# Places moved in a hand-written order of work: visits of attention tiles by one or two products, and three actions of tile 1

## The chip, the cores and the metric

The kernel runs on one core of a Trainium2 chip. The metric is the device time of one execution in microseconds (us), the median of several runs. The engines are TensorE (PE in the profile, its weight loads PEld), VectorE (DVE), ScalarE (ACT), GpSimd (POOL) and SyncE (SP, which here only issues DMAs).

## The reference

Attention over blocks, then a gated feed-forward network (FFN) over all its rows:

```python
batch, n_heads, seq, head_dim = 8, 8, 576, 64      # q, k, v
scores = q @ k.T / sqrt(64)
scores = where(pos_i // 64 >= pos_j // 64, scores, -1e9)   # causal by blocks of 64
attn_out = softmax(scores) @ v

x = attn_out.transpose(0, 2, 1, 3).reshape(4608, 512)
out = (maximum(x @ w_gate, 0) * (x @ w_val)) @ w_out       # 512 -> 1536 -> 512
```

Inputs and output are float32; the kernel works in bfloat16 with sums in float32.

## The kernel before, in words

**Tiles.** Each of the eight batches gives 576 rows of x. The first 512 of a batch are one tile of the FFN (tiles 0 to 7). The last 64 of all batches, their tails, make tile 8.

**FFN.** The generator `ffn_gen` (L931) issues the FFN's matmuls one by one. For each of a tile's 12 blocks of the hidden width there are four products of x with the gate weights (into a PSUM bank `ffnp`), whose relu is done by ScalarE (L947), and four with the value weights (into another `ffnp`), which VectorE multiplies with the relu (`hidden`, L957, tile `hT`). The product with w_out follows. In tiles 0 and 1 it takes 48 matmuls; from tile 2 on it is done by a scheme of seven half-size products, 42 places in place of 48. So a tile is 144 places in tiles 0 and 1, and 138 from tile 2 on: 96 of the gate and value products, then 42. Tile 7's gate and value products are done by a scheme of their own.

**Attention beside it.** While the FFN of tile j runs, the four pairs of heads of batch j + 1 (rounds r = 4b to 4b + 3) are computed between its products. A round has these actions:
- `s`, the *visit* (L431 to L470): the scores of both heads of the pair. They go into two tiles `sc` of two banks each and into a third piece, which is one bank `one` for one head and one bank `ffnp` for the other. The visit begins with this third piece. Then ScalarE makes the exp of the third piece (two instructions, L466) and of the first `sc` (L459).
- `e`: the exp of the second `sc`; `c`: zeros into the corners of the masked blocks (by VectorE in nearly all rounds).
- `a` and `b`: the products with V of the first and the second head (L551), each behind it normalised by VectorE: a reciprocal, a multiplication into `xnat` (L528) and, from batch 3 on, one into `xtail` (L535).
- `x`: `xnat` is transposed into the next tile's `xT`, by a DMA (L633) or, in the first batches, by TensorE through a PSUM bank and a copy (`to_xT_pe`, L625 to L631).

In PSUM there are two `sc` tiles, one bank `one`, and three banks `ffnp`. The gates, the values, the products with V and half of each visit's third piece take turns at the `ffnp` banks.

**Early batches.** Batches 0 to 2 are loaded, cast and transposed by other ways. `cast_tails` (L204) casts tails of k and v from a staging tile into `k_bt` and `v_bf`; `td1` is its part for one half of the heads of batch 1, done by VectorE: one cast of k and one of v. `pe_tails` (`t1`, L289 to L304) transposes the tails of q and k on TensorE. `unpermute` (`u2`, L253 to L257) copies q and k of one pair of heads of batch 2 into their places (`qTm`, `kTm`), here by two VectorE copies. Actions named `q`, `ev`, `tc`, `v2` are GpSimd's casts for these batches; GpSimd issues its own DMAs in between.

**What sets the order.** The program writes all engines' instructions in an order made by hand. The table `AT` (L1325) gives each action a place counted in the FFN's places. The loop at its end sorts the actions by place, lets the FFN run up to the place and then issues the action; an action's instructions thereby get their position on every engine at once. For batches 4 to 7 (which run beside tiles 3 to 6) the places come from `STEADY` (L1608), an offset within a round of 28 places (loop L1701 to L1708). `place_of` (L1735) rounds down and, from tile 2 on, shortens the last 48 places of each 144 to 42.

```python
STEADY = {"s": 2, "e": 8, "c": 15, "a": 22, "b": 26, "x": 26.1}
...
for n in sorted(acts, key=lambda n: AT[n]):
    at = int(place_of(AT[n]))
    ffn(at - place[0])          # FFN matmuls up to here
    place[0] = max(place[0], at)
    acts[n]()                   # then the action
```

Of the kernel before, what the change touches and what calls it, by code (L numbers as in the profile page):

```python
# [17 lines left out]
def kernel(  # L18
# [287 lines left out]
    def load_qkv(b, which, behind=None):  # L306
        for t in which:
            src = (q, k, v)[t]
            for c in range(NCH):
                if (b, 0) not in bfs:  # L310
                    bfs[b, 0], bfs[b, 1] = new_bf(), new_bt()
                here = src[b, :, 128 * c : min(128 * c + 128, S), :]
                if c < 4:
                    dst = (
                        v_bf[b % 2][:, c, :, 0:64]
                        if t == 2
                        else bfs[b, 0][t][:, 512 * c : 512 * c + 512].rearrange(
                            "p (h d) -> p h d", h=8
                        )
                    )  # L320
                    pieces = [(dst, here.rearrange("h p d -> p h d"))]
                elif t == 0:
                    pieces = [
                        (
                            bfs[b, 1].rearrange("p (h d) -> p h d", h=8),
                            here.rearrange("h p d -> p h d"),
                        )
                    ]
                else:
                    pieces = [  # L330
                        (
                            halves_of(v_bf[b % 2][:, 4, :, :], par)[:, :, 0:64]
                            if t == 2
                            else k_bt[b % 2][
                                64 * par : 64 * par + 64, :, 64 * par : 64 * par + 64
                            ],
                            here.rearrange("(h g) p d -> g p h d", g=2)[par],
                        )
                        for par in range(2)
                    ]  # L340
                for dst, part_of in pieces:
                    ins = nc.gpsimd.dma_start(dst, part_of)  # L342
                    after(ins, behind)
                    behind = None
# [3 lines left out]
    def dma_transposes(b):  # L348
        m, tl = bfs[b, 0], bfs[b, 1]
        for t in range(2):  # L350
            nc.sync.dma_start_transpose(
                (qTm, kTm)[t][b % 2].rearrange("p c h n -> p (c h) n"),
                m[t],
            )
        tails_by_dma(b, tl)
# [116 lines left out]
    def last_keys(b):  # L472

        last = psum_one.tile([128, 512], FP, name="one")[:, 0:256]
        for hp in range(4):
            nc.tensor.matmul(
                last[:, 64 * hp : 64 * hp + 64],
                kTt[b % 2][:, hp, :],
                qTt[b % 2][:, hp, :],
                start=True,  # L480
                stop=True,
            )
        nc.scalar.activation(attnL[b % 2][:, 0:256], last, AF.Exp, scale=scale)
# [749 lines left out]
    with tc.manual_schedule(engines={E.PE, E.DVE, E.Activation, E.Pool, E.SP}):  # L1233
# [4 lines left out]
        def round_at(r, how):  # L1238

            exps = []  # L1240

            def begin():
                exps.extend(visit(r))
                exps[0]()
                exps[1]()

            corner, first, second, xT = how
            return {
                f"s{r}": begin,
                f"e{r}": lambda: exps[2](),  # L1250
                f"c{r}": lambda: corners(r, zeros_by[corner]),
                f"a{r}": lambda: head_av(r, 0, first),
                f"b{r}": lambda: head_av(r, 1, second),
                f"x{r}": lambda: (
                    to_xT_pe(r, by[xT[0]], xT[1]) if xT else to_xT_dma(r)
                ),
            }
# [58 lines left out]
        def mains_1(hp):  # L1316
# [8 lines left out]
        AT = {  # L1325
            "Lq0": -63.5,
            "Lq2": -62.27,
            "Lv0": -61.59,
            "Lv2": -59.5,
            "Lq6": -59.5,  # L1330
            "Lq4": -59.5,
            "v00": -58.48,
            "g00": -56.5,
# [104 lines left out]
            "k0": 77.3,  # L1438
            "m0": 84.0,
            "m1": 87.1,  # L1440
            "s4": 93.79,
            "E2v0": 109.09,
            "cw21/1": 110.84,
            "e4": 114.3,
# [22 lines left out]
            "x6": 145.48,  # L1467
            "a7": 147.62,
            "b7": 147.81,
            "x7": 152.01,  # L1470
            "td0": 156.81,
            "t0": 163.43,
            "td1": 164.5,
            "S0": 164.53,
            "t1": 164.55,
            "L0": 165.13,
# [11 lines left out]
            "s8": 198.81,  # L1488
            "e8": 199.59,
            "c8": 207.05,  # L1490
            "u2": 207.72,
            "s9": 208.6,
            "A1": 210.5,
            "o0": 211.5,
# [206 lines left out]
        for b in range(4, B):  # L1701
            base = 144 * (b - 1)
            for i in range(4):
                r = 4 * b + i
                here = ("sc", "sc") if i == 3 else ("one", "ffn")
                acts.update(round_at(r, ("dve", *here, None)))
                for n, p in STEADY.items():
                    AT[f"{n}{r}"] = base + 28 * i + p + (5 if i == 3 and n in "abx" else 0)  # L1708
            acts[f"L{b}"] = lambda b=b: last_keys(b)
            AT[f"L{b}"] = base + 11  # L1710
            if b + 1 < B:
                acts[f"l{b + 1}"] = lambda b=b: load_qkv(b + 1, (0, 1), products[-1])
                acts[f"lv{b + 1}"] = lambda b=b: load_qkv(b + 1, (2,))
                acts[f"d{b + 1}"] = lambda b=b: dma_transposes(b + 1)
                for n, p in (("l", 9), ("lv", 46), ("d", 66)):
                    AT[f"{n}{b + 1}"] = base + p
# [6 lines left out]
        for i in range(15):  # L1723
            n, which = i // 5, (5, 2, 1, 6, 7)[i % 5]
# [52 lines left out]
```

## Time and profile before

| | |
|---|---|
| median of 3 runs | 354.22 us (353.58 to 354.94) |
| the profiled execution, its time | 353.72 us |
| its span in the trace | 351.9 us, granted TensorE clock 0.999 |
| VectorE busy | 224.2 us (64%) |
| ScalarE busy | 185.9 us (53%) |
| GpSimd busy | 154.4 us (44%) |
| gate and value matmuls, L937 | 93.8 and 90.1 us in the two largest groups |
| relu, L947 | 57.3 us, 606 ns each |
| multiplication into hT, L957 | 53.3 us, 684 ns each |

All numbers but the first row are of one execution, taken by the hardware profiler. A row of the timeline reads: start in us from the span's start, busy time in us, engine, line of the kernel, operation, output tile <- input tiles, then the shape, and x with the number of instructions that the row gathers (with several, the busy time is that of all of them). Square brackets at a row's end hold the engine's idle time ahead of the instruction and the instruction that ended it. TensorE's matmuls are pipelined and their ends are modelled, so what can be trusted of a matmul is its start. The busy share of an engine is a mean over a kernel with several stages.

### The profile page before, as it was taken

The page shows a single profiled execution, that of the slowest core. Times are in us where ns is not written, and L with a number is a line of the kernel's source. Part 1 is how long each engine was busy: PE and PEld are TensorE (multiplying, and loading weights), DVE is VectorE, ACT ScalarE, POOL GpSimd, SP SyncE. Part 2 cuts the span into 40 slices and gives each one's busy share as a digit, 9 for nine tenths or more (in the row PEclk, how much of TensorE's full clock was granted, in tenths as well). Part 3 has the DMA queues.
Part 4 walks back from the last instruction along what each step waited for, and adds up shares of the span by engine and source line. Part 5 has one row for each costly group of instructions (what it writes and reads, how often), then busy time and mean ns, then how long its engine had stood idle before and what let it go on. Part 6 is the DMA issues. An engine that isn't in the chain of part 4 may idle for free.

```text
span 351.9 us, 8257 instructions
## 1 busy us (share of the span) xinstructions
PE 340.1 (97%) x3202; PEld 209.3 (59%) x3245; DVE 224.2 (64%) x558; ACT 185.9 (53%) x298; POOL 154.4 (44%) x195
## 2 busy tenths in 40 slices
PE   7899999999999999999999999999999999999994
PEld 2544455545454568555855576557755687687674
DVE  4654455658546784467547772668566867885892
ACT  4942756587335861666355546555366515423521
POOL 4847556588956902590149203950300022213213
PEclk9999999999999999999999999999999999999999
DMA  8999999999999996899459944999310031003005
GB/s 241 295 353 374 345 232 270 199 142 172 186 208 103 144 178 130 113 143 165 65 135 140 145 92 125 129 141 141 114 47 15 18 84 60 2 0 122 1 2 119
DMA packets 155399, 50.02 MB, mean 142 GB/s; under 512 B 134464, under 2 KB 151744, under 8 KB 155360
## 3 DMA queue, kind: packets, MB, share of 16 engines
q0 software_dynamic: 70528, 8.98, 46.8%
q1 hardware_dynamic: 76432, 31.47, 44.5%
q10 hardware_dynamic: 8400, 9.05, 8.2%
q8 instruction: 25, 0.41, 0.5%
q14 instruction: 14, 0.11, 0.1%
HBM read 37.75 MB, written 9.44 MB: 134 GB/s over the span
## 4 chain that ended last, share of the span: by engine, by line
PE 89%; ACT 5%; DVE 2%; issue 1%; POOL 1%; POOLq 0%; DVEq 0%
PE ffnp L937 45%; PE ffnp L819 12%; PE ffnp L1168 5%; PE one L819 5%; PE sc L1003 3%; PE sc L454 3%; ACT attnT L418 3%; PE one L454 2%; PE one L589 2%; PE one L1003 2%; PE ffnp L589 2%; PE one L937 1%; PE ffnp L551 1%; PE sc L589 1%; ACT attnT L459 1%
## 5 line engine op out<-in xcount | busy, mean ns | idle before, releaser
L937 PE MATMUL ffnp<-xT,wg 128*128 128x512 bf16 x340 | 93.8, 379 | 0.8
L947 ACT ACTIVATE gate_sb<-ffnp 128x512 bf16<-128x512 f32 x95 | 57.3, 606 | 70.1 <-PE ffnp L937 65.7
L937 PE MATMUL ffnp<-xT,wv 128*128 128x512 bf16 x315 | 90.1, 379 | 1.6 <-issue 0.6
L957 DVE TENSOR_TENSOR hT<-gate_sb,ffnp 128x512 bf16<-128x512 bf16 x78 | 53.3, 684 | 51.6 <-PE ffnp L937 27.0
L459 ACT ACTIVATE attnT<-sc 128x1024 bf16<-128x1024 f32 x56 | 57.5, 1042 | 0.0
L937 PEld LDWEIGHTS <-wv 128*128 128x128 bf16 x384 | 35.0, 98 | 36.6 <-issue 3.7
L937 PEld LDWEIGHTS <-wg 128*128 128x128 bf16 x384 | 35.3, 98 | 35.6 <-issue 2.2
L871 POOL TENSOR_TENSOR ob<-ob 128x512 f32<-128x512 f32 x7 | 9.6, 1371 | 103.0 <-ACT ob L868 54.2
L819 PEld LDWEIGHTS <-stage 128*128 128x128 bf16 x420 | 40.3, 98 | 6.0
L778 DVE TENSOR_TENSOR stage<-hT 128x512 bf16<-128x512 bf16 (+2 forms) x82 | 37.8, 493 | 0.9
L589 PEld LDWEIGHTS <-attnT 128*128 128x128 bf16 x640 | 26.7, 98 | 12.6 <-issue 1.3
L819 PE MATMUL ffnp<-stage 128*128 128x256 bf16 x252 | 31.4, 273 | 0.0
L466 ACT ACTIVATE attnT<-one 128x512 bf16<-128x512 f32 (+1 forms) x28 | 15.0, 536 | 26.4 <-PE ffnp L454 26.4
L342 POOL DMA_DIRECT2D q_bf<-in_q_dram x20 | 18.2, 921 | 22.4 <-DVE hT L957 17.1
L342 POOL DMA_DIRECT2D v_bf<-in_v_dram x30 | 24.1, 849 | 2.0 <-DMA k_bf<-in_k_dram 0.8
L1168 PE MATMUL ffnp<-wo,hT 128*128 128x512 bf16 x90 | 22.4, 379 | 0.2
L454 PEld LDWEIGHTS <-kTm 64*128 64x128 bf16 x384 | 13.1, 94 | 14.3 <-issue 8.3
L1034 POOL TENSOR_TENSOR ob<-ob 128x512 f32<-128x512 f32 x6 | 7.7, 1275 | 23.2 <-ACT ob L1033 20.2
L454 PE MATMUL sc<-qTm,kTm 64*128 64x512 bf16 (+1 forms) x168 | 17.8, 305 | 0.0
L342 POOL DMA_DIRECT2D k_bf<-in_k_dram x20 | 17.7, 922 | 0.0
L819 PEld LDWEIGHTS <-hT 128*128 128x128 bf16 x168 | 16.4, 98 | 1.9
L868 ACT COPY ob<-ffnp 128x512 f32<-128x512 f32 x7 | 4.1, 585 | 22.1 <-PE ffnp L819 22.1
(192 smaller groups left out, 550.3 us busy)
## 6 DMA issues: line engine op xcount, KB each, us to landing
out_dram<-ob ACTq DMA_DIRECT2D x32, 256.0 KB, 2.4
stage<-in_moe_w_val_dram SPq DMA_DIRECT2D x6, 512.0 KB, 8.3
stage<-in_moe_w_gate_dram SPq DMA_DIRECT2D x6, 512.0 KB, 8.7
stage<-in_moe_w_out_dram SPq DMA_DIRECT2D x6, 512.0 KB, 10.6
q_bf<-in_q_dram POOLq DMA_DIRECT2D x20, 128.0 KB, 4.4
k_bf<-in_k_dram POOLq DMA_DIRECT2D x20, 128.0 KB, 5.9
v_bf<-in_v_dram POOLq DMA_DIRECT2D x20, 128.0 KB, 6.4
stage<-in_v_dram SPq DMA_DIRECT2D x19, 128.0 KB, 5.4
```

Of the source, the lines that this page charges most:

```text
L342: ins = nc.gpsimd.dma_start(dst, part_of)
L454: nc.tensor.matmul(o, kTm[b % 2][head_of(hh), c, hp, :], qT, start=True, stop=True)
L459: return lambda: nc.scalar.activation(at[:, :, lo : lo + 512], sc, AF.Exp, scale=scale)
L466: nc.scalar.activation(at[:, hh, 1024 : 1024 + w], third[hh][:, 0:w], AF.Exp, scale=scale)
L589: nc.tensor.matmul(av[:, p, :], at[:, col : col + 128], v_bf[b % 2][:, c, h, :], start=(p == 0), stop=(c == p), skip_group_check=True,)
L778: nc.vector.tensor_tensor(out=out.rearrange("p (c n) -> p c n", c=m), in0=a, in1=b, op=op)
L819: nc.tensor.matmul(to, sums.of(c)[which][:, 128 * p : 128 * p + 128], right, start=first, stop=(c == 5), skip_group_check=True,)
L937: nc.tensor.matmul(to, (wg, wv)[t][f // 4][:, c, 128 * (f % 4) : 128 * (f % 4) + 128], x[:, c], start=(c == 0), stop=(c == 3),)
L947: nc.scalar.activation(gate_sb, gate, AF.Relu)
L957: nc.vector.tensor_tensor(out=h, in0=gate_sb, in1=val, op=AX.mult)
L1003: nc.tensor.matmul(to[:, 256 * k : 256 * k + 256], left[:, c, 128 * k : 128 * k + 128], right[:, c], start=new and (k, c) == (0, 0), stop= ...
L1168: nc.tensor.matmul(op, hT[f][:, 128 * s : 128 * (s + 1)], wo[f // 4][:, f % 4, n0:n1], start=(f == 0), stop=(f == 11),)
```

## The change

Sixteen actions get another place (twelve visits beside tiles 3 to 6, and four entries of the table); no instruction is added, removed or changed in form.

- `s4`, the first visit beside tile 0: place 93 becomes 95.
- `x7`, the last transpose into tile 1's xT by TensorE: place 152 becomes 153. Its copy to SBUF (VectorE, L631) goes with it.
- `td1`: from place 164 to 157, so that VectorE's two casts stand ahead of two multiplications into hT instead of behind them.
- `u2`: from 207.72 to 208.5. No matmul lies between, but the multiplication into hT whose last product is place 208 now stands ahead of VectorE's two copies.
- the visits of batches 4 to 7: the second and the fourth of each batch come one product later, the third two, the first stays.

```diff
             "m1": 87.1,
-            "s4": 93.79,
+            "s4": 95,
...
-            "x7": 152.01,
+            "x7": 153,
             "td0": 156.81,
             "t0": 163.43,
-            "td1": 164.5,
+            "td1": 157,
             "S0": 164.53,
             "t1": 164.55,
...
-            "u2": 207.72,
+            "u2": 208.5,
             "s9": 208.6,
...
                 for n, p in STEADY.items():
-                    AT[f"{n}{r}"] = base + 28 * i + p + (5 if i == 3 and n in "abx" else 0)
+                    AT[f"{n}{r}"] = base + 28 * i + p
+                    if i == 3 and n in "abx":
+                        AT[f"{n}{r}"] += 5
+                    if n == "s":
+                        AT[f"{n}{r}"] += (0, 1, 2, 1)[i]
```

## The prediction

> **What bounds the kernel now.** I read the page first, its busy shares and its chain.
>
> ```profile
> PE 340.1 (97%) x3202; PEld 209.3 (59%) x3245; DVE 224.2 (64%) x558; ACT 185.9 (53%) x298; POOL 154.4 (44%) x195
> ...
> PE 89%; ACT 5%; DVE 2%; issue 1%; POOL 1%; POOLq 0%; DVEq 0%
> ```
>
> TensorE is busy for 97% of the span and carries 89% of the chain. The change adds and removes no instruction, so it can only gain where TensorE waits. The table of waits hardly shows such places: the ends of matmuls are modelled and overlap, so a wait shorter than that overlap leaves no idle time. It shows in the starts. I therefore went through the timeline and compared starts. Take the visits. A visit begins with two 256-column products on the two halves of the rows, one into the bank `one`, one into an `ffnp` bank. Here is the first visit of tile 3, which the change leaves alone, and then the second, which it moves by one product.
>
> ```profile
> 140.61 0.28 PE L454 MATMUL one<-qTm,kTm 64*128 64x256 bf16 x1
> 140.61 0.28 PE L454 MATMUL ffnp<-qTm,kTm 64*128 64x256 bf16 x1
> ```
>
> ```profile
> 148.38 0.20 DVE L535 TENSOR_TENSOR xtail<-ffnp,recip 64x64 bf16<-64x64 f32 x1
> ...
> 148.56 0.28 PE L454 MATMUL one<-qTm,kTm 64*128 64x256 bf16 x1
> 148.64 0.28 PE L454 MATMUL ffnp<-qTm,kTm 64*128 64x256 bf16 x1
> ```
>
> In the first visit the two start together at 140.61. In the second the `ffnp` product starts 0.08 after the other. What it waits for stands above it: VectorE's last reading of the previous head's sums (the xtail row) ends at 148.38 + 0.20 = 148.58, and the product starts 0.06 later. The bank that the visit takes is the one that those sums lay in.
>
> **The change part by part.**
>
> *Tiles 3 to 6, twelve visits.* The third visit of tile 3, with what follows it, and the last of the twelve (tile 6, fourth visit):
>
> ```profile
> 156.46 0.28 PE L454 MATMUL one<-qTm,kTm 64*128 64x256 bf16 x1
> 156.53 0.28 PE L454 MATMUL ffnp<-qTm,kTm 64*128 64x256 bf16 x1
> ...
> 158.60 1.03 PE L937 MATMUL ffnp<-xT,wg 128*128 128x512 bf16 x4
> 158.82 0.62 ACT L947 ACTIVATE gate_sb<-ffnp 128x512 bf16<-128x512 f32 x1
> ...
> 159.29 1.06 ACT L459 ACTIVATE attnT<-sc 128x1024 bf16<-128x1024 f32 x1
> ...
> 159.49 1.02 PE L937 MATMUL ffnp<-xT,wv 128*128 128x512 bf16 x3
> ...
> 160.20 0.65 ACT L947 ACTIVATE gate_sb<-ffnp 128x512 bf16<-128x512 f32 x1
> ...
> 161.21 0.59 PE L937 MATMUL ffnp<-xT,wv 128*128 128x512 bf16 x2
> ```
>
> ```profile
> 276.60 0.28 PE L454 MATMUL one<-qTm,kTm 64*128 64x256 bf16 x1
> ...
> 276.76 0.28 PE L454 MATMUL ffnp<-qTm,kTm 64*128 64x256 bf16 x1
> ```
>
> Four products start 158.60 to 159.46, so one takes 0.216. One product more in front of the visit covers a wait of 0.08, and of 0.16 too. Of the twelve waits the first (148.56) is 0.08 and the last 0.16; I take 0.075 for each of the eleven, from 0.08 here and 0.07 at 156.46. The sum is 11 x 0.075 + 0.16 = 0.99 us.
>
> The third visit moves by two products, and that changes an order on ScalarE. Now the relu of this gate stands behind the visit's first three exps: it runs 158.82 to 159.44, and the value product that takes its bank, due at 158.60 + 4 x 0.216 = 159.46, starts at 159.49. After the change the gate's last product stands ahead of the visit, the relu ahead of the exps, and this 0.03 goes: 4 x 0.03 = 0.12, a little less by the unrounded starts, 0.11. The price lies behind it: ScalarE now waits for the gate before it can begin the visit's chain. The chain was relu and four exps in either order, and its end moves from 159.29 + 1.06 = 160.35 to about 160.4, while TensorE's products come 0.1 earlier. The next relu (160.20 to 160.85) must end before the value product at 161.21: a cover of 0.36, of which some 0.15 goes. I cost it at nothing. Nothing else is queued behind the moved visits but their own exps, and no DMA is issued by them.
>
> *Tile 0, the first visit of the next batch, two products later.*
>
> ```profile
> 39.82 0.68 DVE L957 TENSOR_TENSOR hT<-gate_sb,ffnp 128x512 bf16<-128x512 bf16 x1
> ...
> 40.24 0.28 PE L454 MATMUL one<-qTm,kTm 64*128 64x256 bf16 x1
> 40.55 0.27 PE L454 MATMUL ffnp<-qTm,kTm 64*128 64x256 bf16 x1
> ```
>
> The same wait, 0.31 less the 0.01 of rounding: VectorE's multiplication ends at 40.50. Two products are 0.43, so all of it goes: 0.30. The visit's exps come 0.1 later; ScalarE has no other work there.
>
> *Tile 1, the last transpose to xT one product later.*
>
> ```profile
> 59.86 0.59 PE L937 MATMUL sc<-xT,wv 128*128 128x512 bf16 x2
> ...
> 60.05 0.43 DVE L528 TENSOR_TENSOR xnat<-one,recip 128x256 bf16<-128x256 f32 x1
> 60.45 0.40 POOL L216 CAST v_bf<-stage 64x256 bf16<-64x256 f32 x1
> ...
> 60.53 0.40 PE L630 MATMUL one<-ident,xnat 128*128 128x128 bf16 x4
> 60.97 0.42 DVE L631 COPY xT<-one 128x512 bf16<-128x512 bf16 x1 [0.49 <-PE one L630]
> ...
> 61.63 0.59 PE L937 MATMUL ffnp<-xT,wg 128*128 128x512 bf16 x2
> ```
>
> Two products from 59.86 end their turn at 60.29; the transposes start at 60.53, just after VectorE's xnat (60.48). So TensorE loses 0.24, and one product moved in fills 0.22 of it. But the products from 61.63 on need the copy to xT, which ends at 61.39 and does not move, as the transposes don't. With one product fewer between, they are due at 61.41 and can start at about 61.44: 0.19 gained, with bounds of 0.1 and 0.24.
>
> *Tile 1, two tail casts earlier.*
>
> ```profile
> 62.67 0.69 DVE L957 TENSOR_TENSOR hT<-gate_sb,ffnp 128x512 bf16<-128x512 bf16 x1 [0.64 <-PE sc L937]
> ...
> 64.35 0.29 DVE L209 CAST k_bt<-stage 64x256 bf16<-64x256 f32 x1
> 64.48 0.28 PE L294 MATMUL ffnp<-ident,q_bt 64*128 64x64 bf16 x4
> ...
> 64.78 0.38 PE L300 MATMUL ffnp<-ident,k_bt 128*128 128x128 bf16 x4
> ```
>
> The transposes of k_bt start 0.14 after their cast ended (64.64). With the cast long done they follow the four before them at once. The gain lies between 0 and 0.14, since part of the 0.14 is the semaphore's way (0.06 above); I take 0.08. The two casts, 0.29 each, fall into VectorE's idle 0.64 ahead of 62.67; without that cover two multiplications would start 0.6 later.
>
> *Tile 1, two copies behind a multiplication.*
>
> ```profile
> 77.26 0.63 ACT L947 ACTIVATE gate_sb<-ffnp 128x512 bf16<-128x512 f32 x1
> ...
> 77.83 0.60 DVE L257 COPY qTm<-perm 128x512 bf16<-128x512 bf16 x1
> ...
> 78.34 0.85 DVE L257 COPY kTm<-perm 128x512 bf16<-128x512 bf16 x1
> ...
> 79.12 0.67 DVE L957 TENSOR_TENSOR hT<-gate_sb,ffnp 128x512 bf16<-128x512 bf16 x1
> ...
> 79.84 0.38 PE L937 MATMUL ffnp<-xT,wv 128*128 128x512 bf16 x1
> ```
>
> ```profile
> 80.68 0.77 DVE L216 CAST v_bf<-stage 64x256 bf16<-64x256 f32 x1
> ...
> 82.30 0.42 DVE L528 TENSOR_TENSOR xnat<-one,recip 128x256 bf16<-128x256 f32 x1
> ...
> 82.79 0.28 PE L454 MATMUL one<-qTm,kTm 64*128 64x256 bf16 x1
> ```
>
> Now the value product at 79.84 waits for the multiplication (79.79), which stood behind the copies. That wait, about 0.21 (one product), goes. But VectorE works without a pause from 77.83 to 82.72, and the visit at 82.79 starts 0.07 after its xnat: it is bound by VectorE already. In the new order the multiplication must wait for the relu (77.89) and starts at about 77.94, where the copy started at 77.83. The chain, 0.11 longer, ends 0.11 later, and so does the visit. What was gained at 79.84 is waited for at 82.79, and 0.11 more: a loss of 0.11.
>
> A row for a doubt: of the two copies of one form, one took 0.60 and one 0.85. The Trainium skill, "SBUF — State Buffer", section "Who interferes with whom", says that a VectorE copy in a two-port mode and a GpSimd instruction lock each other out of a shared port pair for a whole instruction. By it the two copies and the casts behind them would meet other moments of GpSimd, and stretch anew or less. The profile shows the stretch, not its cause.
>
> **Sum.** 0.99 + 0.11 + 0.30 + 0.19 + 0.08 - 0.11 = 1.56 us. The profiled execution took 353.72 (span 351.9), the median of the runs is 354.22. From the one I come to 352.16, from the other to 352.66; I forecast the middle, **352.4**. From there on to the end TensorE is the bound, so nothing gives the gain back.
>
> **The rivals.**
> 1. *VectorE's pieces in tile 1 come out shorter.* If the copy takes 0.60 and the cast at 80.68 its fellows' 0.29, the chain is 0.73 shorter, the visit at 82.79 no longer waits, and the copies' move gains 0.21 instead of losing 0.11: 1.88, 352.1. For it: the same forms show the shorter times. Against: they met GpSimd's stream of DMA issues then and will again. 0.15.
> 2. *They come out longer*: the first copy 0.25 and the k cast 0.48 more, as their fellows. The visit starts 0.73 later: a gain of 0.83, 353.1. 0.10.
> 3. *The third visit's chain on ScalarE runs late.* If it ends 0.3 later than I reckon, the value product at 161.21 waits 0.15 and perhaps the corner writes behind it: 4 x 0.15 = 0.6 back, 353.0. Against: the cover of 0.36. 0.10.
> 4. *Slower than before.* VectorE takes its work in order, and the moved casts read batch 1's tails. GpSimd read the same load's other half at 60.45, so it had landed. If it lands later than about 62.0 in another execution, VectorE stands, and with it both multiplications, the copy to kTt and TensorE behind their banks, one for one. Beyond 62.0 + 1.56 = 63.6 the change loses; a landing 4.2 us later than now would give 354.9, 0.5 above the middle of the two bases. In the old order the casts stood at 64.35 and hid it. 0.05.
>
> That the edits don't act as they say is excluded by the instruction order: TensorE's differs in just these places.
>
> **How the numbers follow.** The forecast (a gain of 1.3 to 1.9) gets 0.60. Its own range is 351.9 to 352.9. The range over all takes in rivals 1 to 3 and the half microsecond between the two bases: 351.6 to 353.5; what it leaves out is rival 4 and the tails of the runs. 0.5% is 1.77 us, about what a measurement of this kernel can tell from no change. The forecast lies just short of it; about a third of its chance (0.21) and nearly all of rival 1's (0.14) lie beyond: faster 0.35. Rival 4 gives slower 0.05. The rest is within: 0.60.
>
> **What would show it.** In the changed profile `one` and `ffnp` start together in all sixteen visits; the starts 40.24 and 40.55 fall together; the tile's third relu of that kind ends ahead of the visit's exps; the transposes of the last xT follow the products without a gap; the visit at 82.79 still starts right after VectorE's xnat. Wrong would be a new gap of starts at the value products behind the third visits, or a VectorE idle "DMA stage" ahead of the casts at 62.

## The result and the profile after

| | before | changed |
|---|---|---|
| median of 6 runs each | 354.09 us (353.58 to 355.00) | 352.15 us (352.11 to 353.06) |
| the profiled execution, its time and span | 353.72, 351.9 | 352.94, 351.2 |
| ratio of the times | | 0.9949, 95% interval 0.9929 to 0.9969 |

The gain of the medians is 1.94 us; the ratio of 0.9949 is a gain of 0.51%, just at the bound that the prediction set itself. The time is 0.25 below the forecast of 352.4. Four of the six runs lie between 352.11 and 352.17; forecast from the profiled execution was 352.16. The profiled execution is one of the two that took 0.9 more. Two lines of its page, the busy shares and the chain that ended last, show what is new:

```profile
PE 341.7 (97%) x3245; PEld 207.2 (59%) x3245; DVE 224.8 (64%) x558; ACT 185.7 (53%) x298; POOL 153.8 (44%) x195
...
PE 90%; ACT 3%; DMA 3%; DVE 2%; POOL 1%; issue 0%; POOLq 0%
```

TensorE is as busy as before (of its matmuls, 43 have no record in the profile before: 3202 in place of 3245), but a DMA now has 3% of the chain, where none stood before. The rest shows in starts. From the timeline of the changed kernel, the moved visits: tile 0's, the second of tile 3, the last of tile 6.

```profile
40.68 0.28 PE L454 MATMUL one<-qTm,kTm 64*128 64x256 bf16 x1
40.68 0.28 PE L454 MATMUL ffnp<-qTm,kTm 64*128 64x256 bf16 x1
...
148.67 0.21 DVE L535 TENSOR_TENSOR xtail<-ffnp,recip 64x64 bf16<-64x64 f32 x1
...
149.07 0.28 PE L454 MATMUL one<-qTm,kTm 64*128 64x256 bf16 x1
149.07 0.28 PE L454 MATMUL ffnp<-qTm,kTm 64*128 64x256 bf16 x1
...
276.21 0.28 PE L454 MATMUL one<-qTm,kTm 64*128 64x256 bf16 x1
276.22 0.28 PE L454 MATMUL ffnp<-qTm,kTm 64*128 64x256 bf16 x1
```

Each pair of products now starts together. VectorE's last reading of the bank (the xtail row) ends at 148.88, 0.19 ahead of the visit and no longer 0.06. The third visit of tile 3, same timeline:

```profile
157.11 0.28 PE L454 MATMUL ffnp<-qTm,kTm 64*128 64x256 bf16 x1
157.22 0.60 ACT L947 ACTIVATE gate_sb<-ffnp 128x512 bf16<-128x512 f32 x1 [1.59 <-PE ffnp L937]
...
157.71 0.59 ACT L466 ACTIVATE attnT<-one 128x512 bf16<-128x512 f32 x1
...
158.66 1.96 ACT L459 ACTIVATE attnT<-sc 128x1024 bf16<-128x1024 f32 x2
158.75 1.03 PE L937 MATMUL ffnp<-xT,wg 128*128 128x512 bf16 x4
159.62 1.03 PE L937 MATMUL ffnp<-xT,wv 128*128 128x512 bf16 x4
...
161.34 0.60 PE L937 MATMUL ffnp<-xT,wv 128*128 128x512 bf16 x2
```

The relu is ahead of the visit's exps, and the value product at 159.62 follows four gate products after 0.87, that is 4 x 0.216: no wait. The later one at 161.34 has none either.

The stages compare by the start of the same product in both profiles. The first visit of tile 3, which does not move, starts at 140.61 before and at 140.91 after: +0.30. The spans end at 351.94 and 351.16: -0.78. So tiles 3 to 6 gave 1.08 us. Ahead of them the shift after each edit is -0.30 (s4), -0.48 (x7), -0.56 (td1), -0.69 (u2), and then this happens at tile 2's first products:

```profile
101.00 0.60 PE L937 MATMUL ffnp<-xT,wg 128*128 128x512 bf16 x2
102.43 0.59 PE L937 MATMUL ffnp<-xT,wg 128*128 128x512 bf16 x2 [0.83 <-DMA xT<-xnat]
```

The third product needs the third chunk of xT, whose DMA transpose landed late. It starts 1.43 after the first two began, instead of 0.43: 1.0 us lost, and -0.69 became +0.30. In the kernel before the four products ran without a gap:

```profile
101.69 1.03 PE L937 MATMUL ffnp<-xT,wg 128*128 128x512 bf16 x4
```

### The profile page after: what moved, and what is told of

The parts are those of the page before. It is cut to its first block, busy times and chain, and to the rows that moved or that the text cites. A ratio compares the mean times of both kernels' runs of the same rounds, so it can differ in the third digit from the quotient of the medians.

```text
span 351.2 us, 8299 instructions
## 1 busy us (share of the span) xinstructions
PE 341.7 (97%) x3245; PEld 207.2 (59%) x3245; DVE 224.8 (64%) x558; ACT 185.7 (53%) x298; POOL 153.8 (44%) x195
## 4 chain that ended last, share of the span: by engine, by line
PE 90%; ACT 3%; DMA 3%; DVE 2%; POOL 1%; issue 0%; POOLq 0%
PE ffnp L937 46%; PE ffnp L819 12%; PE one L819 5%; PE ffnp L1168 4%; PE sc L1003 3%; PE sc L454 3%; DMA xT<-xnat 3%; ACT attnT L418 3%; PE one L454 2%; PE ffnp L589 2%; PE one L589 2%; PE one L1003 2%; PE one L937 1%; PE sc L589 1%; PE ffnp L551 1%; PE one L1219 1%
## 5 line engine op out<-in xcount | busy, mean ns | idle before, releaser
L937 PE MATMUL ffnp<-xT,wg 128*128 128x512 bf16 x356 | 96.8, 380 | 0.9 <-DMA xT<-xnat 0.8
L937 PE MATMUL ffnp<-xT,wv 128*128 128x512 bf16 x336 | 93.0, 380 | 0.0
L1168 PE MATMUL ffnp<-wo,hT 128*128 128x512 bf16 x96 | 23.7, 380 | 0.0
L454 PEld LDWEIGHTS <-kTm 64*128 64x128 bf16 x384 | 11.0, 95 | 15.2 <-issue 8.5
L454 PE MATMUL sc<-qTm,kTm 64*128 64x512 bf16 (+1 forms) x168 | 16.8, 305 | 0.0
```

Source lines behind the costliest of these rows:

```text
L454: nc.tensor.matmul(o, kTm[b % 2][head_of(hh), c, hp, :], qT, start=True, stop=True)
L937: nc.tensor.matmul(to, (wg, wv)[t][f // 4][:, c, 128 * (f % 4) : 128 * (f % 4) + 128], x[:, c], start=(c == 0), stop=(c == 3),)
L1168: nc.tensor.matmul(op, hT[f][:, 128 * s : 128 * (s + 1)], wo[f // 4][:, f % 4, n0:n1], start=(f == 0), stop=(f == 11),)
```

## The experiments

Each kernel is given as a diff to the changed kernel, unless said otherwise. All were run beside the kernel before.

**The visits alone.** The kernel before, with the loop's new lines only.

```diff
+                    if n == "s":
+                        AT[f"{n}{r}"] += (0, 1, 2, 1)[i]
```

> Only the twelve visits of tiles 3 to 6 move; tiles 0 and 1 stay as before. Theory (each moved visit had waited for VectorE's last reading of the bank it takes): 1.1 us faster than before, and in the trace the products one and ffnp of all sixteen visits start together, while the waits of tiles 0 and 1 (0.31 at the first visit, 0.24 ahead of the last transposes, 0.21 ahead of a value product) stand as before. Rival (the twelve visits gain by what ScalarE does earlier or later, not by the bank): no equal steps of 0.07 to 0.09 per visit, another sum. A late landing of tile 2's xT (it cost the changed kernel's profiled execution 1.0 us) may add up to 1 us in some executions here too, as it may in the kernel before.

12 runs, median 352.87 us (352.62 to 354.75), before 353.93: 1.06 faster, ratio 0.9975 (0.9963 to 0.9986). In the trace the visits start together, and each moved visit takes 0.07 to 0.09 off the shift against the kernel before, the last 0.16. The theory holds, and the sum too. The profiled execution is the slowest of the twelve, and shows something that the prediction had not seen:

```profile
79.26 0.95 DVE L257 COPY kTm<-perm 128x512 bf16<-128x512 bf16 x1 [0.70 <-DMA perm<-k_bf]
...
80.14 0.67 DVE L957 TENSOR_TENSOR hT<-gate_sb,ffnp 128x512 bf16<-128x512 bf16 x1
...
80.86 1.02 PE L937 MATMUL ffnp<-xT,wv 128*128 128x512 bf16 x4 [0.93 <-DVE hT L957]
```

In the old place of u2 the second copy waited for the landing of its perm tile (79.24; in the kernel before 77.35, a microsecond before it was read). The multiplication waited behind it, and TensorE behind that: 1.09 lost where the kernel before lost 0.21.

**The four places alone.** The kernel before, with s4, x7, td1 and u2 moved.

```diff
-            "s4": 93.79,
+            "s4": 95,
...
-            "x7": 152.01,
+            "x7": 153,
...
-            "td1": 164.5,
+            "td1": 157,
...
-            "u2": 207.72,
+            "u2": 208.5,
```

> Only the four entries of the table move (s4, x7, td1, u2); the visits of tiles 3 to 6 stay. By the forecast 0.46 us faster than before, by the two traces 0.69 (0.30 + 0.18 + 0.10 + 0.13 behind the copies, for which -0.11 was forecast). Theory on the late landing of tile 2's xT, that TensorE's earlier arrival lays bare: some executions lose up to 0.7 more than in the kernel before. Rival, that it varies by itself: as many late executions in the kernel before as here.

11 runs, median 353.45 (352.93 to 354.41), before 353.93: 0.48 faster, ratio 0.9982 (0.9973 to 0.9991). It lies by the forecast's 0.46, and the fastest runs differ by 0.62. The two halves add up: 1.06 + 0.48 = 1.54. The profiled execution has no wait at tile 2's xT, so TensorE's earlier arrival does not bring it about in every execution. The times of the kernel before spread as widely (353.55 to 355.26), which speaks for the rival but does not prove it.

**All but the copies.**

```diff
-            "u2": 208.5,
+            "u2": 207.72,
```

> The whole change but the move of the two copies u2. Forecast: these copies lose 0.11, so this is 0.11 faster than the changed kernel (gain 1.67). By the trace of the changed kernel they gain 0.13 (a cast behind them took 0.54 in place of 0.77): 0.13 slower than it (gain about 1.43). If the cast's length varies by itself from execution to execution, the cast here takes something other than 0.77; if the copies' place sets it, 0.77 again.

8 runs, median 352.83 (352.06 to 353.98), ratio 0.9965 (0.9953 to 0.9977). That does not tell 0.1 us either way. The profile does more: perm landed at 78.83, the copy of kTm waited 0.77, TensorE lost 1.21 at the value product; this execution, 353.98, is the slowest of the eight. The cast of v_bf behind them took 0.29. So its length is not set by the copies' place alone.

**What stretches VectorE's copies and casts.** In the profiles so far the stretched ones have one thing in common: they end just after a DMA issue of GpSimd. From the changed kernel's timeline:

```profile
79.74 0.95 POOL L342 DMA_DIRECT2D k_bf<-in_k_dram  x1
80.23 0.54 DVE L216 CAST v_bf<-stage 64x256 bf16<-64x256 f32 x1
```

The issue ends at 80.69, the cast at 80.77. In the kernel before it was an issue of 80.45 to 81.34 and the cast's end at 81.45. To take this away, GpSimd's loads were tied to a later multiplication:

```diff
-            "l3": 217.2,
+            "l3": 222.5,
...
-            "l3": lambda: load_qkv(3, (0, 1)),
+            "l3": lambda: load_qkv(3, (0, 1), products[-1]),
```

> The changed kernel with GpSimd's loads of q and k for batch 3 issued behind VectorE's multiplication before the visit at 82 us, so that GpSimd issues nothing while VectorE does u2's copies and the casts of batch 2's tails. Theory (a VectorE copy or cast that meets GpSimd's DMA issue ends only about 0.1 or 0.3 after that instruction's end): the copy of kTm takes 0.60 in place of 0.85, the cast of v_bf 0.29 in place of 0.54 to 0.77, and the visit of the third pair starts 0.07 earlier. Rival (the two differ by form or address): the lengths stay 0.85 and above 0.5. The whole kernel may be slower, as batch 3's loads come 6 us later; only the lengths and that visit count here.

```profile
78.66 0.62 DVE L257 COPY qTm<-perm 128x512 bf16<-128x512 bf16 x1
79.19 0.60 DVE L257 COPY kTm<-perm 128x512 bf16<-128x512 bf16 x1
...
80.68 0.29 DVE L216 CAST v_bf<-stage 64x256 bf16<-64x256 f32 x1
...
82.01 2.80 POOL L342 DMA_DIRECT2D q_bf<-in_q_dram  x3 [6.48 <-DVE recip L526]
...
82.71 0.28 PE L454 MATMUL one<-qTm,kTm 64*128 64x256 bf16 x1
```

With GpSimd still, the copy takes 0.60 and the cast 0.29, and the visit follows its products without a wait. The theory holds; the instructions and their order are the same as before. The Trainium skill, "SBUF — State Buffer", section "Who interferes with whom", says that of a VectorE instruction in a two-port mode and a GpSimd instruction the one that comes second is blocked for the whole of the first. The order agrees with it, though no view shows the mode in which these copies and casts run. Its two ends do not quite, and there the rows decide. The thirteen stretched casts between 70 and 100 us in all profiles, 0.29 long by themselves, end 0.09 to 0.12 after the issue's recorded end, as if they had been let in some 0.2 before. And a cast that begins 0.17 to 0.19 after an issue's start takes 0.29 (four profiles), one that begins 0.23 after it 0.77 (the kernel before), as if the issue did not shut VectorE out in its first 0.2. The whole took 355.74 in its one run: batch 3's loads come 6 us later, and tile 2 waits 0.16 and 1.71 for xT.

**The third visit by one product.**

```diff
-                        AT[f"{n}{r}"] += (0, 1, 2, 1)[i]
+                        AT[f"{n}{r}"] += (0, 1, 1, 1)[i]
```

> The changed kernel with the third visit of tiles 3 to 6 one product later in place of two. By the prediction's step (one product of 0.216 covers a bank wait of 0.07, and the second only brings the relu ahead of the exps, 0.03 for each tile): 0.1 slower than the changed kernel, the value product behind the visit again 0.03 late. Rival (the wait of the bank is longer than one product): a gap of starts at the visits, 0.3 or more slower. Rival (the relu's place costs as much as it gives): no difference.

12 runs, median 353.72 (352.91 to 354.87); the changed kernel on the same chip 352.98. That is 0.74 slower by the medians and 0.75 by the fastest runs. In the timeline of tile 3:

```profile
157.02 0.28 PE L454 MATMUL ffnp<-qTm,kTm 64*128 64x256 bf16 x1
...
158.88 1.03 PE L937 MATMUL ffnp<-xT,wg 128*128 128x512 bf16 x4
159.33 0.62 ACT L947 ACTIVATE gate_sb<-ffnp 128x512 bf16<-128x512 f32 x1
...
160.00 1.02 PE L937 MATMUL ffnp<-xT,wv 128*128 128x512 bf16 x4
```

The visit starts together, but the relu still stands behind its exps. It ends at 159.95, and the value product starts at 160.00, 1.12 after the gate's first in place of 0.87: by the shift against the changed kernel 0.25 lost in each of the four tiles, 0.98 in all. The times differ by less, 0.74; what gave the rest back is not known. The expectation of 0.03 forgot that the exps themselves come one product later while the product that needs the relu's bank does not: 0.03 + 0.216 is the 0.25. So the second product is not a small extra: without it the third visit's move would cost more than it brings.

**GpSimd's loads of v later.**

```diff
-            "lv3": 224,
+            "lv3": 262,
```

> The whole change, and GpSimd's loads of v for batch 3 (lv3) moved from place 224 to 262, behind the transposes to tile 2's xT and behind GpSimd's first sums of weights. Theory: these loads, spread over all DMA queues at 97 to 103% of the engines' time between 84 and 106 us, hold up the DMA transposes of xT, whose landing at 102.39 in place of about 101.3 cost 1.0 us. Without them the transposes land within some 3 us of their issue, all executions lie at about 352.1 and none at 353.0. Rival (the transposes are slow by themselves, or behind the output's DMAs): they still take 7 us or more to land, and late executions stay.

12 runs, median 353.89 (352.17 to 357.01): no better, and spread wider. The test failed in its making: GpSimd came to these loads at 92.0 to 96.8, just when the transposes were in flight (issued at 92.58 and 95.18, landed 7.1 and 7.0 later). It did not separate the two.

**Tile 2 takes the late chunks later.**

```diff
+            if j == 2:
+                first = 2
+                acc = {
+                    n: psum_ffn.tile([128, 512], FP, name="ffnp")
+                    for n in ((0, 0), (1, 0), (0, 1))
+                }
+                order = [(t, f, c) for t, f in acc for c in (0, 1)]
+                order += [(t, f, c) for t, f in acc for c in (2, 3)]
+                order += [(1, 1, c) for c in range(4)]
...
             for f in range(first, 12):
```

> The changed kernel, and tile 2's first two blocks of the hidden width take the first two chunks of x for two gates and one value before any of them takes the third chunk, so that six products lie ahead of the first use of the third chunk in place of two. Theory (the executions above the floor wait there for the DMA transposes of xT): the same floor, 352.1, and a late landing costs up to 0.86 us less (four products of 0.216), so the executions at 353.0 go or come down to about 352.3. Rival (they lose elsewhere): as many executions near 353.0 as in the changed kernel. A bank that the third accumulator takes earlier may cost 0.1 to 0.3 at the start of tile 2.

8 runs, median 352.91 (352.21 to 355.63); the changed kernel beside it 352.98 (352.16 to 354.15). The floor is the same, and the slower executions do not go. In the profile TensorE waits 0.08 for the bank of the third accumulator and 0.26 ahead of tail products at 103.75. So the wait at tile 2 is not the whole of what varies.

**The changed kernel again**, twice.

> The changed kernel once more, for its executions' times beside those of the next two kernels on the same chip. Theory: what varies are the landings of DMAs (tile 2's xT near 102 us, the perm tiles near 78 us), so the times fall into a floor at 352.1 and executions up to 1 us above it, median between 352.1 and 353.0.

12 runs, median 352.98 (352.16 to 354.15), before 354.22, ratio 0.9961 (0.9942 to 0.9980). The profiled execution, at 352.95, has no wait for xT. It began the FFN 0.65 later than the first profile, from its start-up, and lost more on VectorE's chain near 80 us:

```profile
78.62 0.88 DVE L257 COPY qTm<-perm 128x512 bf16<-128x512 bf16 x1
...
79.43 0.76 DVE L257 COPY kTm<-perm 128x512 bf16<-128x512 bf16 x1
...
81.08 0.67 DVE L216 CAST v_bf<-stage 64x256 bf16<-64x256 f32 x1
...
83.08 0.28 PE L454 MATMUL one<-qTm,kTm 64*128 64x256 bf16 x1
```

Copies and cast meet GpSimd's issues at other moments: 0.88, 0.76 and 0.67, where the first profile had 0.61, 0.85 and 0.54. TensorE lost 0.20 at a gate product near 80.8 and 0.19 at this visit, 0.39 together. In the first profile it was 0.07, in the kernel before 0.21.

> The changed kernel, to stand beside the three others of this call on the same chip: floor 352.1 to 352.2, median 352.1 to 353.0.

12 runs, median 352.63 (351.95 to 355.40), before 354.23, ratio 0.9957 (0.9940 to 0.9975).

**A late perm, made on purpose, with u2 in the old and in the new place.** Both have the first line, the old one the second as well.

```diff
-            "q24": 191.07,
+            "q24": 191.5,
...
-            "u2": 208.5,
+            "u2": 207.72,
```

> The changed kernel but with u2 in its old place, and GpSimd's casts that the transposes to perm wait for (q24) put behind its two casts of v, so that perm lands some 0.7 to 1.5 us later in every execution. Theory (the old place lets VectorE stand at the copy of kTm while the multiplication waits behind it): TensorE loses 0.5 to 1.5 at the value product near 79 us in place of 0.2, as the executions of the kernels without u2's move did (1.1 and 1.2), and the time is about 1 above that of late_perm_new or nearly so. Rival (u2 only trades places within one chain of VectorE): the same loss in both, only at another place.

> The changed kernel whole, u2 in its new place, with the same later perm as in late_perm_old. Theory: the multiplication runs ahead of the wait, nothing is lost near 79 us, and the copies' wait comes back at the visit near 82 us, less the 0.55 that the copies start later: a loss smaller by 0.3 to 0.6 than that of late_perm_old. Rival (one chain): the same total, within 0.1.

The old place first, then the new one:

```profile
79.55 0.59 DVE L257 COPY kTm<-perm 128x512 bf16<-128x512 bf16 x1 [1.31 <-DMA perm<-k_bf]
...
80.79 1.02 PE L937 MATMUL ffnp<-xT,wv 128*128 128x512 bf16 x4 [1.62 <-DVE hT L957]
```

```profile
79.49 0.68 DVE L257 COPY kTm<-perm 128x512 bf16<-128x512 bf16 x1 [0.97 <-DMA perm<-k_bf]
...
80.77 0.39 PE L937 MATMUL ffnp<-xT,wg 128*128 128x512 bf16 x1 [0.74 <-DVE xtail L567]
...
103.06 0.38 PE L937 MATMUL ffnp<-xT,wg 128*128 128x512 bf16 x1 [0.69 <-DMA xT<-xnat]
104.66 0.38 PE L937 MATMUL ffnp<-xT,wg 128*128 128x512 bf16 x1 [1.22 <-DMA xT<-xnat]
```

Perm landed at 79.52 and 79.47, 2.3 later than in the changed kernel's three profiles (77.1 to 77.2) and not the 0.7 to 1.5 that was meant. The old place lost 1.78 by starts, the new one 0.90 and nothing at the visit: it covers 0.87, more than the 0.3 to 0.6 expected. But the times do not show the gain: medians 353.88 (353.04 to 354.76 and one of 358.06, 10 runs) and 354.50 (353.66 to 356.62, 10 runs), against the kernel before 1.0000 (0.9976 to 1.0024) and 1.0015 (0.9997 to 1.0033). The intervals overlap, so neither place is shown to be the faster as a whole; the expected gain of about 1 us did not come. In the new one's profile, one of its slower executions (355.80), TensorE came to tile 2 earlier and stood there twice for xT, 0.85 and 1.39 by starts, against 0.19 and 0.14 with the old. What was gained near 80 us was waited for at 103, and more; the fourth chunk itself landed 1.0 later than with the old place (104.61 and 103.58), so an earlier TensorE is not the whole of it.

**The casts of batch 2's tails earlier, the copies behind the tails' normalisation.**

```diff
-            "u2": 208.5,
+            "u2": 210.6,
...
-            "td2": 214.72,
+            "td2": 206.9,
```

> The changed kernel with two more moves on VectorE: the casts of batch 2's tails (td2, 0.83 to 1.06 with the stretch) into its idle time near 76 us, ahead of the multiplication at 77, and u2's copies behind the normalisation of batch 1's tails. Theory (the visit at 82 us is bound by VectorE's chain since the casts meet GpSimd's issue): that visit waits no longer; 0.07 faster than the changed kernel where its chain is short, 0.3 to 0.4 where the copies and the casts are stretched (its second profile), so about 0.2 in the median. Rival (the casts wait for the tails' landing, 74.6 to 76.2, ahead of a multiplication): up to 0.5 slower in late executions.

```profile
79.44 0.59 DVE L257 COPY qTm<-perm 128x512 bf16<-128x512 bf16 x1
79.47 1.56 POOL L342 DMA_DIRECT2D k_bf<-in_k_dram  x1
79.95 0.60 DVE L257 COPY kTm<-perm 128x512 bf16<-128x512 bf16 x1
...
82.06 0.28 PE L454 MATMUL one<-qTm,kTm 64*128 64x256 bf16 x1
```

12 runs, median 352.21 (351.67 to 355.17), ratio to before 0.9952 (0.9935 to 0.9969). Beside it the changed kernel had 352.63 (351.95 to 355.40): 0.42 faster by the medians, 0.28 by the fastest runs. TensorE has no wait left between 78 and 83 us, and none at tile 2; in this execution it stood 0.80 for tile 3's xT instead. Here it was VectorE that came first, and GpSimd's issue took 1.56 in place of 0.9. The two kernels were not compared by an interval of their own, and their runs overlap widely, so the 0.42 is not shown. Its fastest run, 351.67, is the lowest of all.

## Why the prediction was right, and where it was not

- **Tiles 3 to 6: right.** Forecast 0.99 + 0.11 = 1.10, measured 1.08 by starts and 1.06 by the kernel that has only these. The profile of that kernel shows the same steps. That the relu's place is the point of the third visit's second product was shown too; what it prevents, 0.25 for each tile, is some eight times the 0.03 that the prediction counted as its gain, and is no part of the sum only because the change does not do it by halves.
- **s4: right**, 0.30 for 0.30. **x7: right**, 0.18 for 0.19. In the same timeline the transposes start 0.24 after the product that the change puts in front of them, where a product takes 0.216, and one product fewer stands behind them:

```profile
60.00 0.38 PE L937 MATMUL ffnp<-xT,wg 128*128 128x512 bf16 x1
60.24 0.40 PE L630 MATMUL one<-ident,xnat 128*128 128x128 bf16 x4
```

- **td1: right**, 0.08 to 0.10 for 0.08. The tails' landing, the rival that would have made it slower, was not met: in the fourteen profiles they landed between 60.0 and 62.1, where the casts were moved at 61.5 or before, and the moved casts stood at 61.69 or later. The rival's own sum has a slip: 354.9 is 0.9 above the middle of the two bases (353.97), not 0.5. The forecast does not use it.
- **u2: the mis-sized term.** The prediction had -0.11: a chain on VectorE, 0.11 longer by the order. In the profiled execution it was +0.13:

```profile
77.37 0.69 DVE L957 TENSOR_TENSOR hT<-gate_sb,ffnp 128x512 bf16<-128x512 bf16 x1
...
78.49 0.85 DVE L257 COPY kTm<-perm 128x512 bf16<-128x512 bf16 x1
...
81.62 0.42 DVE L528 TENSOR_TENSOR xnat<-one,recip 128x256 bf16<-128x256 f32 x1
...
82.10 0.28 PE L454 MATMUL one<-qTm,kTm 64*128 64x256 bf16 x1
```

  The order is as forecast, and the visit still starts at the end of VectorE's xnat. But the chain's length is set by which issue of GpSimd each copy and cast meets. In seven profiles with u2 in its new place and perm on time (the changed kernel's three, and those of the four places, late v loads, third visit by one and split blocks), TensorE lost 0 to 0.42 there, against 0.21 before. Against that one profile of the old place u2's effect lies between +0.21 and -0.21. Rival 1's gain of 0.21 came once, with the four places (no wait at the visit, though the cast took 0.70). Rival 2's direction came in three of the seven, with 0.32 to 0.42 lost, but never near its size: at most 0.21 more than before, where it priced 0.73. Besides this the old place had a price that the prediction missed, the wait for perm: 1.09 and 1.21 in two profiles of kernels that kept it. Both are the slowest executions of their kernels, so how often it is paid is not known.
- **The number: inside its range, and in part by luck.** The base was not off: the middle of 353.72 and 354.22 is 353.97, and the kernel before had 354.09 beside the changed one. But the gain of these six runs, 1.94, is above the forecast's 1.56, and the two repeats gave 1.24 and 1.60, on both sides of it. Over the three sets together the medians are 354.22 (67 executions before) and 352.74 (30 of the changed kernel), 1.48 apart, and the fastest are 353.55 and 351.95, 1.60 apart. Four of the first six lay near 352.1, where the sum from the profile lies too; in the repeats five of 24 were below 352.3. No execution of the changed kernel near 352.1 was profiled, so what u2 did in them is not known.
- **"Nothing gives the gain back": wrong as a rule.** It was said of TensorE from the visit at 82.79 to the end. A landing at tile 2 took back 1.0 in the first profile of the changed kernel, 0.82 in the third, nothing in the second. In tile 2 the kernels with only the four places and with the earlier casts had no such wait, the one with only the visits had 0.91. What moves these landings from execution to execution is not settled: the late loads of v fell on the transposes all the same, and splitting the first blocks did not lift the median. Whether the change makes the wait more frequent stays open too.

## What to carry to other kernels

On a busy TensorE, look for waits in the starts: two products that should start together, or four that should take 4 x 0.216, show 0.07 us that no idle time shows, and one product moved in front pays it. When an action is moved, go through every engine that it issues on: the third visit pays by the place of a relu on ScalarE, and by one product less it would have lost. Where TensorE's waits are gone, the landings of DMAs and VectorE's meetings with GpSimd are what is left; there a gain of 0.1 us can't be forecast from one execution.

## What the runs showed of the hardware that was not expected

- A VectorE copy or cast in SBUF and a DMA issue on GpSimd hold each other up, and either can be the one that waits: the cast of 64x256 took 0.29 alone and up to 0.77 beside an issue of 0.89; an issue took 1.56 beside two copies of 0.60. What decides is small: a cast that began 0.17 to 0.19 after the issue's start went through, one that began 0.23 after it waited. Stretched copies of 128x512 end 0.28 to 0.32 after the issue's recorded end, in all twenty cases between 70 and 100 us.
- DMA transposes to xT took 5.4 to 9.9 us from issue to landing between 85 and 105 us. That of tile 2's third chunk alone took 7.8 in the kernel with the four places and 9.9 in the changed one, which issue it at the same point of the program.
